# Turned queries and keys share the PSUM banks of the values; the values are spread over four units; the third pair's raw rows get a buffer

## The chip, the cores and the metric

The kernel runs on one core of one Trainium2 chip. The metric is device time in microseconds (us), the median of several executions; lower is better. TensorE is called PE here, VectorE DVE, ScalarE ACT, GpSimd POOL, and SyncE, which only issues DMAs, SP.

## The reference

Attention over 2 batches and 8 heads, 576 positions, head width 64, all fp32, with a bias made by a small network from the logarithmic distance of two positions; its output goes through a feed-forward layer with a rational activation and then through four experts. The change touches attention alone.

```
scores = scale * matmul(q, k.T)                # 16 (batch, head) pairs of 576 x 576
h = maximum(x @ w1 + b1, 0)                    # x from the distances, 32 hidden units
scores = scores + (h @ w2)                     # one bias per head
attn = exp(scores - max); attn /= sum
x = matmul(attn, v)                            # 576 x 64 for each (batch, head)
h = x @ w_in; g = P(h) / (Q(h) + 1e-6); x = g @ w_out
out = sum over 4 experts of p_e * (relu(x @ w1_e) @ w2_e)
```

## The kernel before

**Stages.** By the trace, the bias tables are made until 59 us of the span, attention runs from there to about 209 us, and the two feed-forward layers fill the rest. Everything is in an order written out by hand; each engine works through its own queue in that order, and waits only on semaphores.

**Attention** goes over 8 pairs of heads, n = 0 to 7. In a pair there are nine units, u = 0 to 8: a unit is 128 rows of scores of one head, and u = 8 holds the last 64 rows of both. For each unit PE makes scores (`sc`, line 453; units 2k and 2k+1 together), DVE adds the bias and takes the row extreme (`pq`, `nm`, line 457), ACT takes the exponential (line 466), and DVE turns the result in 32 x 32 blocks into `pt` (line 473). Scores run two units ahead of the turning. The values of pair n-1 (`o <- pt, val`, line 506, 18 blocks of 32 keys, 16 matmul records each) are made while pair n is at work, from `fill(n, u)`.

**PSUM.** `ps` has two tiles of two banks each, used in turn by all scores (one tile for each head of units 2k and 2k+1, one for u = 8) and by `rt`, the turned reciprocal sums (`turn`, lines 486 to 494), which ACT copies to `rs`. `po` has one tile of four banks, handed out by `big()`: once to `prep(n)`, which turns the raw queries and keys of pair n on PE (lines 172 to 181), and once to the values of a pair. Both take the same four banks by turns: a new owner waits until the old one's readers are done. `prep` puts its two ACT copies, to `ks` and `qs`, in the list `soon`, which runs after the turning in the next unit. `qs` and `ks` have two buffers each, so those of pair n+2 take the place of those of pair n. `divide` copies the finished values out of PSUM with three ACT instructions; `put` multiplies and splits them on POOL.

**Where these stand in pair n** (for n above 1): values at u = 1, 3 and 5, six blocks each; `divide` at u = 5; `turn` at u = 6; `prep(n + 2)` at u = 7, which at once has SP load the raw rows of pair n+3 into the single buffers `raw_q` and `raw_k`; `load_v(n + 1)` at u = 6 and the three copies of it within SBUF at u = 1 of the next pair. Pair 1 has 7, 7 and 4 blocks at u = 3, 5 and 6, and `prep(3)` at u = 8. `prep(1)` stands in pair 0 and `prep(2)` in pair 1 at u = 1; units 6 and 7 of pair 0 come after unit 1 of pair 1.

**SP's queue** is first in, first out. While the bias is made it takes the first pair's rows, the values, the second pair's rows, and then 32 transfers of the bias (`ba <- ev`, line 246); the rows of the third pair (`load_qk(2)`, issued by `prep(1)`) stand behind these.

**The feed-forward weights** of the first layer begin to be narrowed during pairs 4 to 7: three DVE instructions, two of ACT and one of POOL for each of four pieces.

Of the kernel before, what the change touches and what calls it, by code (L numbers as in the profile page):

```python
# [11 lines left out]
F32 = mybir.dt.float32  # L12
F32R = mybir.dt.float32r
U32 = mybir.dt.uint32
AF = mybir.ActivationFunctionType
# [3 lines left out]
B, H, S, D = 2, 8, 576, 64  # L19
# [6 lines left out]
P = 128  # L26
# [6 lines left out]
NKB = S // 32  # L33
# [14 lines left out]
def attention_then_two_ffn(ctx: ExitStack, tc: tile.TileContext, q, k, v, w1, b1, w2, w_in, w_out, ca, cb, probs, e_w1, e_w2, c_l, c_l8, c_p, c_x, out):  # L48
    nc = tc.nc
    act, dve, pool, pe, sp = nc.scalar, nc.vector, nc.gpsimd, nc.tensor, nc.sync  # L50
# [13 lines left out]
    ident = const.tile([P, P], F32, name="ident")  # L64
# [9 lines left out]
    def blk(slot, shape, dt, name):  # L74
        return long.tile(shape, dt, tag=f"blk{slot}", name=name)

    ps = ctx.enter_context(tc.tile_pool(name="ps", bufs=2, space=PSUM))
# [61 lines left out]

    raw_q = rp.tile([P, 5, 2, D], F32, name="raw_q")  # L140
    raw_k = rp.tile([P, 5, 2, D], F32, name="raw_k")
    val = [rp.tile([P, 2 * NKB, D], F32, tag=f"v{i}", name="val") for i in range(2)]

    def load_qk(n):

        p, b = divmod(n, 2)
        for x, y in ((raw_q, q), (raw_k, k)):
            h = y[b, 2 * p:2 * p + 2]
            for e in range(2):
                sp.dma_start(x[:, 0:4, e], h[e, 0:512].rearrange("(t p) d -> p t d", p=P))  # L150
            sp.dma_start(x[0:64, 4], h[:, 512:S].rearrange("e r d -> r e d"))
# [17 lines left out]
        for f in now:  # L169
            f()  # L170

    def turned(x, tp):
        for t in range(5):
            m = P if t < 4 else 64
            pe.transpose(tp[:, t * P:t * P + m], x[:m, t].rearrange("p e d -> p (e d)"), ident[:m, :m])  # L175

    def turn_q(n, tp):
        turned(raw_q, tp)

    def turn_k(n, tk):  # L180
        turned(raw_k, tk)

    def copy_q(n, tp):
        q_of[n] = qs = qk.tile([P, S], F32, tag="qs", name="qs")
        act.activation(qs, tp[:, :S], AF.Copy, scale=0.125)

    def copy_k(n, tk):
        k_of[n] = ks = qk.tile([P, S], F32, tag="ks", name="ks")
        act.activation(ks, tk[:, :S], AF.Copy)

    def prep_q(n, tp):
        turn_q(n, tp)
        copy_q(n, tp)

    def prep_k(n, tk):
        turn_k(n, tk)
        copy_k(n, tk)

    def two_banks():
        return ps.tile([P, 1024], F32, tag="s", name="tp_qk")  # L200

    bias = {}

# [60 lines left out]
    load_qk(0)  # L264
    load_v(0, 4)
    BESIDE = {0: cut_near, 2: lambda: inverse_psi(psi), 5: cut_far}
    BESIDE.update({6: lambda: prep_q(0, two_banks()), 7: lambda: (prep_k(0, two_banks()), load_qk(1))})
    for r in range(4):
        dve.tensor_scalar(wb[:, r], w2c, pick[:, 3 - r:4 - r], None, ALU.mult)
    for m in range(AHEAD):  # L270
# [151 lines left out]

    sums_z = ap.tile([P, P], F32, name="sums_z", bufs=1)

    def big():
        return po.tile([P, 4, 512], F32, tag="o", name="o")

    def prep(n):
        o = big().rearrange("p a j -> p (a j)")
        turn_q(n, o[:, 0:1024])  # L430
        turn_k(n, o[:, 1024:2048])
        if n + 1 < NN:
            load_qk(n + 1)
        soon.append(lambda: (copy_k(n, o[:, 1024:2048]), copy_q(n, o[:, 0:1024])))

    soon = []

    class Pair:
# [57 lines left out]
        def values(self, blocks):  # L496

            if blocks[0] == 0:
                self.o = big()
            for b in blocks:  # L500
                for a in range(4):
                    r = slice(32 * a, 32 * a + 32)
# [73 lines left out]
            act.activation(abs_b[:, j:j + 1], cb_sb[:, j:j + 1], AF.Abs, scale=WUP ** -(j + 1))  # L576
        dve.memset(one, 1.0 + 1e-6)

    VALUES = {1: range(0, 6), 3: range(6, 12), 5: range(12, NKB)}
    FIRST_VALUES = {3: range(0, 7), 5: range(7, 14), 6: range(14, NKB)}  # L580

    def fill(n, u):

# [1 line left out]
        turns = VALUES if n > 1 else FIRST_VALUES  # L585
        if old and u == 6:
            old.turn()
        if old and u in turns:
            old.values(turns[u])
        if old and u == max(turns):  # L590
# [4 lines left out]
            prep(1)  # L595
        if (n, u) == (1, 1):
            prep(2)
        if u == (7 if n > 1 else 8) and 0 < n < NN - 2:
            prep(n + 2)
        if u == 6 and 0 < n < NN - 1:  # L600
            load_v(n + 1)
        if (n, u) in COPY_V:
            copy_v(COPY_V[n, u])
# [283 lines left out]
```

## Time and profile before

| | before |
|---|---|
| median of 3 runs | 819.83 us (818.36 to 822.34) |
| the profiled execution, its own time | 817.92 us |
| its span on the core | 816.1 us |
| PE busy | 781.3 us, 96% |
| DVE busy | 463.3 us, 57% |
| ACT busy | 373.8 us, 46% |
| POOL busy | 132.0 us, 16% |

The span is the time from the first to the last instruction on the core; 1.8 us of the execution's own time lie around it. Shares over the span mix stages: DVE is nearly full until 400 us and almost idle later. A PE row covers a run of matmul records; each fp32 matmul leaves two. A row's end is modelled, and the next row begins before it ends. In square brackets stand the engine's idle time ahead of a row and what ended it; "issue" there means that nothing in the profile held the engine.

### The profile page before, as it was taken

The page shows a single profiled execution, that of the slowest core. Times are in us where ns is not written, and L with a number is a line of the kernel's source. Part 1 is how long each engine was busy: PE and PEld are TensorE (multiplying, and loading weights), DVE is VectorE, ACT ScalarE, POOL GpSimd, SP SyncE. Part 2 cuts the span into 40 slices and gives each one's busy share as a digit, 9 for nine tenths or more (in the row PEclk, how much of TensorE's full clock was granted, in tenths as well). Part 3 has the DMA queues.
Part 4 walks back from the last instruction along what each step waited for, and adds up shares of the span by engine and source line. Part 5 has one row for each costly group of instructions (what it writes and reads, how often), then busy time and mean ns, then how long its engine had stood idle before and what let it go on. Part 6 is the DMA issues. An engine that isn't in the chain of part 4 may idle for free.

```text
span 816.1 us, 15405 instructions
## 1 busy us (share of the span) xinstructions
PE 781.3 (96%) x6550; PEld 679.7 (83%) x6550; DVE 463.3 (57%) x707; ACT 373.8 (46%) x568; POOL 132.0 (16%) x111
## 2 busy tenths in 40 slices
PE   8996988988999999999989999999999999999998
PEld 5443766657899999999989989989899899898997
DVE  7986778787899999999963113322243112321211
ACT  6985555673798879886643113302022021210100
POOL 0000222343244546641200000000000000000000
PEclk9998899999999999999999999999999999999999
DMA  8898576542132233401213002200022000201001
GB/s 143 195 225 182 116 168 144 120 117 76 53 104 83 74 105 102 152 3 53 78 27 103 1 26 78 78 27 1 27 91 78 14 1 31 73 1 39 13 27 39
DMA packets 62179, 62.58 MB, mean 77 GB/s; under 512 B 36736, under 2 KB 45312, under 8 KB 61440
## 3 DMA queue, kind: packets, MB, share of 16 engines
q1 hardware_dynamic: 61680, 61.60, 28.4%
q8 instruction: 51, 0.84, 0.5%
q14 instruction: 16, 0.13, 0.1%
q10 hardware_dynamic: 432, 0.01, 0.0%
HBM read 42.43 MB, written 2.36 MB: 55 GB/s over the span
## 4 chain that ended last, share of the span: by engine, by line
PE 63%; DVE 14%; ACT 6%; issue 5%; POOL 2%; DMA 0%; SPq 0%; ACTq 0%; DVEq 0%; POOLq 0%
PE hp L56 26%; PE op L56 24%; PE sc L56 5%; PE o L506 5%; PE yp L56 2%; DVE qd L692 2%; DVE u L693 2%; DVE narrow L362 2%; DVE narrow L360 2%; DVE u L694 1%; PE o L175 1%; DVE hp L702 1%; DVE qd L701 1%; POOL wi L367 1%; ACT u L690 1%
## 5 line engine op out<-in xcount | busy, mean ns | idle before, releaser
L56 PE MATMUL hp<-x,wi 128*128 128x384 f32 x1656 | 295.6, 338 | 5.3 <-DVE u L703 4.9
L56 PEld LDWEIGHTS hp<-x,wi 128*128 128x128 f32 x1656 | 288.9, 189 | 8.9 <-issue 5.3
L56 PE MATMUL op<-w,h_hi 128*128 128x512 f32 (+1 forms) x592 | 178.5, 384 | 0.0
L772 ACT ACTIVATE h_hi<-hp 128x768 fp32r<-128x768 f32 x48 | 39.0, 812 | 246.6 <-PE hp L56 246.6
L773 DVE SCALAR_TENSOR_TENSOR h_lo<-hp,h_hi 128x768 fp32r<-128x768 f32 x48 | 46.0, 958 | 156.2 <-ACT h_hi L772 156.2
L56 PEld LDWEIGHTS op<-w,h_hi 128*128 128x128 f32 x592 | 110.0, 188 | 21.1
L56 PE MATMUL op<-w,h_lo 128*128 128x512 f32 (+1 forms) x296 | 113.7, 384 | 0.0
L56 PE MATMUL yp<-g_hi,w 128*128 128x384 f32 x384 | 102.1, 336 | 0.4 <-ACT y L756 0.4
L830 DVE SCALAR_TENSOR_TENSOR acc<-op,pr_sb,acc 128x512 f32<-128x512 f32 (+1 forms) x28 | 20.5, 732 | 112.9 <-PE op L56 112.9
L466 ACT ACTIVATE pq<-pq,nm 128x576 f32<-128x576 f32 x72 | 55.4, 770 | 38.1 <-DVE nm L457 37.8
L56 PEld LDWEIGHTS yp<-g_hi,w 128*128 128x128 f32 x384 | 69.7, 188 | 1.3 <-ACT y L756 0.7
L457 DVE CUSTOM_DVE_ANT_0 pq<-sc,ba 128x576 f32<-128x576 f32 x72 | 51.7, 750 | 30.4 <-PE sc L56 30.2
L56 PE MATMUL sc<-ks,qs 64*128 64x288 f32 (+1 forms) x320 | 60.6, 448 | 6.6 <-DVE nm L457 3.8
L56 PEld LDWEIGHTS op<-w,h_lo 128*128 128x128 f32 x296 | 55.6, 188 | 11.2
L56 PE MATMUL yp<-g_lo,w 128*128 128x384 f32 x192 | 64.2, 334 | 0.0
L506 PE MATMUL o<-pt,val 32*64 32x128 f32 (+1 forms) x2304 | 51.5, 307 | 9.9 <-issue 7.2
L506 PEld LDWEIGHTS o<-pt,val 32*64 32x64 f32 x2304 | 42.6, 137 | 20.3 <-issue 14.9
L683 POOL TENSOR_TENSOR g_lo<-u,g_hi 128x768 fp32r<-128x768 f32 x24 | 45.3, 1889 | 68.2 <-ACT g_hi L682 53.7
L56 PEld LDWEIGHTS sc<-ks,qs 64*128 64x128 f32 (+1 forms) x320 | 32.4, 185 | 24.7 <-DVE nm L457 10.7
L473 DVE STREAM_TRANSPOSE pt<-pq 128x576 f32<-128x576 f32 x72 | 52.5, 755 | 0.1
L233 PE MATMUL bps<-hid,wb 128*32 128x288 f32 x576 | 46.9, 410 | 3.8 <-DVE hid L222 2.9
L222 DVE TENSOR_SCALAR hid<-tab,cut 128x576 f32<-128x576 f32 x112 | 48.4, 516 | 0.0
(95 smaller groups left out, 793.2 us busy)
## 6 DMA issues: line engine op xcount, KB each, us to landing
stage<-in_moe_w_dram SPq DMA_DIRECT2D x32, 512.0 KB, 3.5
ba<-ev SPq DMA_DIRECT2D x32, 288.0 KB, 5.2
words<-in_moe_w_in_dram SPq DMA_DIRECT2D x8, 1024.0 KB, 5.6
words<-in_moe_w_out_dram SPq DMA_DIRECT2D x8, 1024.0 KB, 5.0
val<-val SPq DMA_DIRECT2D x21, 288.0 KB, 4.5
val<-in_v_dram SPq DMA_DIRECT2D x11, 288.0 KB, 4.1
raw_q<-in_q_dram SPq DMA_DIRECT2D x16, 128.0 KB, 2.9
raw_k<-in_k_dram SPq DMA_DIRECT2D x16, 128.0 KB, 2.9
```

Of the source, the lines that this page charges most:

```text
L56: pe.matmul(o, lhsT=l, rhs=r, start=start, stop=stop)
L222: dve.tensor_scalar(tiles[par], win, at, 0.0, ALU.add, ALU.max)
L233: pe.matmul(sc[32 * par:32 * par + 32, hf, :288], lhsT=wb.rearrange("p r h -> p (r h)"), rhs=tiles[par][:, 288 * hf:288 * hf + 288], start ...
L360: dve.scalar_tensor_tensor(out=u, in0=lo, scalar=29, in1=u, op0=ALU.logical_shift_right, op1=ALU.bitwise_or)
L457: dve.tensor_tensor_reduce(out=self.row(u + e).rearrange("p (a j) -> p a j", a=2), in0=o[:, :, :288], in1=bs.rearrange("p (a j) -> p a j", ...
L466: act.activation(self.row(u), self.row(u), AF.Exp, bias=least.pop((self.n, u)), scale=-1.0, accum_out=self.sm[:, u:u + 1])
L473: dve.transpose(self.pt[:, 5 * e + k], self.row(u))
L506: pe.matmul(self.o[64 * e:64 * e + 64, a, c:c + 32 * m], lhsT=val[self.n % 2][r, NKB * e + b], rhs=self.pt[r, i:i + m, 32 * b:32 * b + 32] ...
L683: pool.tensor_tensor(lo, u, f32(hi), ALU.subtract)
L772: act.activation(hi, h, AF.Relu)
L773: dve.scalar_tensor_tensor(out=lo, in0=h, scalar=0.0, in1=f32(hi), op0=ALU.max, op1=ALU.subtract)
L830: dve.scalar_tensor_tensor(out=acc[:, j, cols], in0=op, scalar=pr_sb[:, j, e:e + 1], in1=acc[:, j, cols], op0=ALU.mult, op1=ALU.add)
```

## The change

**PSUM.** The four banks of `po` become one tile `ob` for the whole of attention. The values keep columns 0 to 191 of each bank. The queries turned by `prep` go to columns 192 to 447 of banks 0 and 1, the keys to the same columns of banks 2 and 3, and the last 64 rows of each to columns 448 to 511 of banks 0 and 1. A matmul's start flag counts for a bank, so the transposes of pairs 3 and above, made while values are being summed there, carry none.

**Copies.** Queries and keys lie in two banks each, so `copied` takes three ACT instructions for each (256, 256 and 64 columns) where there was one of 576.

**Order.** Values stand at u = 1, 3, 5 and 7 with 5, 5, 3 and 5 blocks; in pair 1 at u = 3, 5 and 7 with 6, 4 and 8. `divide` moves with the last of them to u = 7, `prep(n + 2)` from u = 7 (pair 1: 8) to u = 5, ahead of that unit's values; `load_v(n + 1)` moves from u = 6 to u = 8.

**The third pair.** Its raw rows get a buffer of their own, `raw_2` (in a block of SBUF that later holds a part of attention's output), and `load_qk(2)` is issued right behind `load_qk(1)`, in the bias stage.

```diff
@@ -139,12 +139,17 @@
 
     raw_q = rp.tile([P, 5, 2, D], F32, name="raw_q")
     raw_k = rp.tile([P, 5, 2, D], F32, name="raw_k")
+    raw_2 = blk(10, [P, 2, 5, 2, D], F32, "raw_2")
+
+    def raw(n):
+        return (raw_2[:, 0], raw_2[:, 1]) if n == 2 else (raw_q, raw_k)
+
     val = [rp.tile([P, 2 * NKB, D], F32, tag=f"v{i}", name="val") for i in range(2)]
 
     def load_qk(n):
 
         p, b = divmod(n, 2)
-        for x, y in ((raw_q, q), (raw_k, k)):
+        for x, y in zip(raw(n), (q, k)):
             h = y[b, 2 * p:2 * p + 2]
             for e in range(2):
                 sp.dma_start(x[:, 0:4, e], h[e, 0:512].rearrange("(t p) d -> p t d", p=P))
@@ -169,35 +174,28 @@
         for f in now:
             f()
 
-    def turned(x, tp):
-        for t in range(5):
+    def turned(x, parts, start=True):
+        for t, out in enumerate(parts):
             m = P if t < 4 else 64
-            pe.transpose(tp[:, t * P:t * P + m], x[:m, t].rearrange("p e d -> p (e d)"), ident[:m, :m])
-
-    def turn_q(n, tp):
-        turned(raw_q, tp)
-
-    def turn_k(n, tk):
-        turned(raw_k, tk)
-
-    def copy_q(n, tp):
-        q_of[n] = qs = qk.tile([P, S], F32, tag="qs", name="qs")
-        act.activation(qs, tp[:, :S], AF.Copy, scale=0.125)
-
-    def copy_k(n, tk):
-        k_of[n] = ks = qk.tile([P, S], F32, tag="ks", name="ks")
-        act.activation(ks, tk[:, :S], AF.Copy)
-
-    def prep_q(n, tp):
-        turn_q(n, tp)
-        copy_q(n, tp)
-
-    def prep_k(n, tk):
-        turn_k(n, tk)
-        copy_k(n, tk)
-
-    def two_banks():
-        return ps.tile([P, 1024], F32, tag="s", name="tp_qk")
+            pe.matmul(out, lhsT=x[:m, t].rearrange("p e d -> p (e d)"), rhs=ident[:m, :m], is_transpose=True, start=start, stop=True, skip_group_check=True)
+
+    def copied(x, tp, tail, scale):
+        for a in range(2):
+            act.activation(x[:, 256 * a:256 * a + 256], tp[:, a], AF.Copy, scale=scale)
+        act.activation(x[:, 512:S], tail, AF.Copy, scale=scale)
+
+    def qs_tile(n):
+        q_of[n] = qk.tile([P, S], F32, tag="qs", name="qs")
+        return q_of[n]
+
+    def ks_tile(n):
+        k_of[n] = qk.tile([P, S], F32, tag="ks", name="ks")
+        return k_of[n]
+
+    def prep_first(x, to, scale):
+        tp = ps.tile([P, 1024], F32, tag="s", name="tp_qk")
+        turned(x, [tp[:, t * P:min(S, (t + 1) * P)] for t in range(5)])
+        act.activation(to, tp[:, :S], AF.Copy, scale=scale)
 
     bias = {}
 
@@ -264,7 +262,7 @@
     load_qk(0)
     load_v(0, 4)
     BESIDE = {0: cut_near, 2: lambda: inverse_psi(psi), 5: cut_far}
-    BESIDE.update({6: lambda: prep_q(0, two_banks()), 7: lambda: (prep_k(0, two_banks()), load_qk(1))})
+    BESIDE.update({6: lambda: prep_first(raw_q, qs_tile(0), 0.125), 7: lambda: (prep_first(raw_k, ks_tile(0), 1.0), load_qk(1), load_qk(2))})
     for r in range(4):
         dve.tensor_scalar(wb[:, r], w2c, pick[:, 3 - r:4 - r], None, ALU.mult)
     for m in range(AHEAD):
@@ -422,16 +420,15 @@
 
     sums_z = ap.tile([P, P], F32, name="sums_z", bufs=1)
 
-    def big():
-        return po.tile([P, 4, 512], F32, tag="o", name="o")
+    ob = po.tile([P, 4, 512], F32, tag="o", name="o")
 
     def prep(n):
-        o = big().rearrange("p a j -> p (a j)")
-        turn_q(n, o[:, 0:1024])
-        turn_k(n, o[:, 1024:2048])
-        if n + 1 < NN:
+        q_tail, k_tail = ob[:, 0, 448:512], ob[:, 1, 448:512]
+        for x, a, tail in zip(raw(n), (0, 2), (q_tail, k_tail)):
+            turned(x, [ob[:, a + t // 2, 192 + P * (t % 2):320 + P * (t % 2)] for t in range(4)] + [tail], n < 3)
+        if 1 < n < NN - 1:
             load_qk(n + 1)
-        soon.append(lambda: (copy_k(n, o[:, 1024:2048]), copy_q(n, o[:, 0:1024])))
+        soon.append(lambda: (copied(ks_tile(n), ob[:, 2:4, 192:448], k_tail, 1.0), copied(qs_tile(n), ob[:, 0:2, 192:448], q_tail, 0.125)))
 
     soon = []
 
@@ -496,7 +493,7 @@
         def values(self, blocks):
 
             if blocks[0] == 0:
-                self.o = big()
+                self.o = ob[:, :, 0:192]
             for b in blocks:
                 for a in range(4):
                     r = slice(32 * a, 32 * a + 32)
@@ -576,8 +573,8 @@
             act.activation(abs_b[:, j:j + 1], cb_sb[:, j:j + 1], AF.Abs, scale=WUP ** -(j + 1))
         dve.memset(one, 1.0 + 1e-6)
 
-    VALUES = {1: range(0, 6), 3: range(6, 12), 5: range(12, NKB)}
-    FIRST_VALUES = {3: range(0, 7), 5: range(7, 14), 6: range(14, NKB)}
+    VALUES = {1: range(0, 5), 3: range(5, 10), 5: range(10, 13), 7: range(13, NKB)}
+    FIRST_VALUES = {3: range(0, 6), 5: range(6, 10), 7: range(10, NKB)}
 
     def fill(n, u):
 
@@ -585,6 +582,8 @@
         turns = VALUES if n > 1 else FIRST_VALUES
         if old and u == 6:
             old.turn()
+        if u == 5 and 0 < n < NN - 2:
+            prep(n + 2)
         if old and u in turns:
             old.values(turns[u])
         if old and u == max(turns):
@@ -595,9 +594,7 @@
             prep(1)
         if (n, u) == (1, 1):
             prep(2)
-        if u == (7 if n > 1 else 8) and 0 < n < NN - 2:
-            prep(n + 2)
-        if u == 6 and 0 < n < NN - 1:
+        if u == 8 and 0 < n < NN - 1:
             load_v(n + 1)
         if (n, u) in COPY_V:
             copy_v(COPY_V[n, u])
```

SP at the end of the bias stage, before. `raw_q` and `raw_k` are the raw rows, `ba` the bias, `ev` its source; the first four rows load pair 1, the last two begin pair 2:

```order
L150 DMA raw_q<-in_q_dram 128x4x64 x2
L151 DMA raw_q<-in_q_dram 64x2x64
L150 DMA raw_k<-in_k_dram 128x4x64 x2
L151 DMA raw_k<-in_k_dram 64x2x64
L246 DMA ba<-ev 128x1x576 x32
L150 DMA raw_q<-in_q_dram 128x4x64 x2
L151 DMA raw_q<-in_q_dram 64x2x64
```

The same place after; `raw_151` is the new buffer:

```order
L155 DMA raw_q<-in_q_dram 128x4x64 x2
L156 DMA raw_q<-in_q_dram 64x2x64
L155 DMA raw_k<-in_k_dram 128x4x64 x2
L156 DMA raw_k<-in_k_dram 64x2x64
L155 DMA raw_151<-in_q_dram 128x4x64 x2
L156 DMA raw_151<-in_q_dram 64x2x64
L155 DMA raw_151<-in_k_dram 128x4x64 x2
L156 DMA raw_151<-in_k_dram 64x2x64
L244 DMA ba<-ev 128x1x576 x32
```

The six transfers of pair 2 have moved from behind the 32 of the bias to ahead of them.

PE from unit 8 of pair 2 into pair 3, before: the scores of u = 8, `rt`, the first scores of pair 3, the turned rows of pair 4, the next scores, then values:

```order
L56 MATMUL sc<-ks,qs 64x288 x4
L491 MATMUL rt<-ident,rb 128x128 x4
L56 MATMUL rt<-fold,sums_z 128x64
L56 MATMUL sc<-ks,qs 128x288 x4
L175 MATMUL o<-ident,raw_q 128x128 x4
L175 MATMUL o<-ident,raw_q 128x64
L175 MATMUL o<-ident,raw_k 128x128 x4
L175 MATMUL o<-ident,raw_k 128x64
L56 MATMUL sc<-ks,qs 128x288 x4
L506 MATMUL o<-pt,val 64x160
```

The same place after:

```order
L503 MATMUL o<-pt,val 64x160
L56 MATMUL sc<-ks,qs 64x288 x4
L488 MATMUL rt<-ident,rb 128x128 x4
L56 MATMUL rt<-fold,sums_z 128x64
L56 MATMUL sc<-ks,qs 128x288 x4
L503 MATMUL o<-pt,val 64x160
L503 MATMUL o<-pt,val 64x128
```

Between the first two scores of a pair now stand five blocks of values, and the transposes have gone to the far side of u = 8.

ACT over the same place, before (`x_1528` is what `divide` writes, `pq` the exponential):

```order
L519 ACTIVATE x_1528<-o 128x4x4x32
L519 ACTIVATE x_1528<-o 64x64 x2
L466 ACTIVATE pq,sm<-pq,nm 128x576
L494 ACTIVATE rs<-rt 128x576
L466 ACTIVATE pq,sm<-pq,nm 128x576 x2
L189 ACTIVATE ks<-o 128x576
L185 ACTIVATE qs<-o 128x576
```

and after:

```order
L184 ACTIVATE ks<-o 128x256 x2
L185 ACTIVATE ks<-o 128x64
L184 ACTIVATE qs<-o 128x256 x2
L185 ACTIVATE qs<-o 128x64
L491 ACTIVATE rs<-rt 128x576
L463 ACTIVATE pq,sm<-pq,nm 128x576
L516 ACTIVATE x_1592<-o 128x4x4x32
L516 ACTIVATE x_1592<-o 64x64 x2
```

The copies to `ks` and `qs` have moved ahead of the copy to `rs`, and the three copies of `divide` behind it.

## Rows read from the trace of the kernel before

**Rows 1.** PE around `prep(2)`: start, us, line, output, count, idle before.

```profile
74.81 0.83 PE L175 MATMUL o<-ident,raw_q 128*128 128x128 f32 x5 [1.75 <-DMA raw_q<-in_q_dram]
77.35 1.38 PE L175 MATMUL o<-ident,raw_k 128*128 128x128 f32 x5 [1.71 <-DMA raw_k<-in_k_dram]
...
81.62 2.96 PE L56 MATMUL sc<-ks,qs 64*128 64x288 f32 x8 [0.86 <-DVE nm L457]
84.51 3.36 PE L506 MATMUL o<-pt,val 32*64 32x160 f32 x112
```

**Rows 2.** SP from the bias stage on, same columns.

```profile
28.09 41.11 SPq L246 DMA_DIRECT2D ba<-ev  x32
69.31 3.19 SPq L150 DMA_DIRECT2D raw_q<-in_q_dram  x2
```

**Rows 3.** DVE around `prep(2)` and at the end of attention.

```profile
74.38 1.43 DVE L473 STREAM_TRANSPOSE pt<-pq 128x576 f32<-128x576 f32 x2
80.80 0.76 DVE L457 CUSTOM_DVE_ANT_0 pq<-sc,ba 128x576 f32<-128x576 f32 x1 [4.99 <-PE sc L56]
...
194.28 2.35 DVE L473 STREAM_TRANSPOSE pt<-pq 128x576 f32<-128x576 f32 x3
```

**Rows 4.** Windows: busy us of each engine, granted PE clock, DMA share, GB/s.

```profile
77.40:87.00 9.60, 8.74 (x104) 6.41 (x108) 5.81 (x14) 4.45 (x10) 1.02 (x3) 0.50 0.58 124
109.60:126.40 16.80, 14.52 (x344) 10.47 (x344) 12.83 (x30) 10.05 (x25) 4.82 (x8) 1.00 0.67 165
139.40:141.60 2.20, 0.00 (x1) 0.00 (x0) 2.19 (x5) 0.52 (x2) 0.00 (x0) 0.99 0.00 0
141.60:143.70 2.10, 2.08 (x44) 1.64 (x46) 0.00 (x0) 0.08 (x1) 0.00 (x0) 0.50 0.04 8
163.00:179.00 16.00, 14.59 (x344) 10.15 (x344) 14.09 (x33) 11.05 (x26) 6.52 (x9) 1.00 0.47 122
196.70:199.60 2.90, 2.86 (x80) 2.50 (x80) 1.80 (x4) 0.00 (x0) 2.46 (x4) 0.50 0.03 6
```

**Rows 5.** PE in pairs 2 to 4.

```profile
99.31 1.91 PE L506 MATMUL o<-pt,val 32*64 32x160 f32 x96 [1.05 <-ACT qs L185]
...
118.29 1.24 PE L56 MATMUL sc<-ks,qs 64*128 64x288 f32 x8 [1.95 <-DVE pt L473]
...
124.39 1.19 PE L56 MATMUL sc<-ks,qs 64*64 64x288 f32 x8
...
126.44 1.94 PE L56 MATMUL sc<-ks,qs 64*128 64x288 f32 x8
...
131.24 1.91 PE L506 MATMUL o<-pt,val 32*64 32x160 f32 x96 [0.25 <-ACT qs L185]
```

**Rows 6.** ACT in pair 3.

```profile
126.45 0.65 ACT L494 ACTIVATE rs<-rt 128x576 f32<-128x576 f32 x1
...
130.00 0.65 ACT L189 ACTIVATE ks<-o 128x576 f32<-128x576 f32 x1 [0.29 <-PE o L175]
130.55 0.64 ACT L185 ACTIVATE qs<-o 128x576 f32<-128x576 f32 x1
```

**Rows 7.** ACT's groups by shape: busy us, mean ns, idle before.

```profile
L749 ACT ACTIVATE yacc<-yp 128x384 f32<-128x384 f32 x12 | 4.8, 488 | 0.0
...
L519 ACT ACTIVATE x<-o 64x64 f32<-64x64 f32 x14 | 3.0, 212 | 0.1
```

**Rows 8.** PE's waits from 84 to 200 us: total us, times, longest.

```profile
PE o L506 <- issue: 7.2, 5, 2.4
```

**Rows 9.** DMA queues from 138.09 to 141.62 us: packets, MB, share.

```profile
q1 hardware_dynamic: 32, 0.15, 20.2%
q8 instruction: 1, 0.02, 1.6%
```

**Rows 10.** PE at the end of attention.

```profile
190.53 1.91 PE L506 MATMUL o<-pt,val 32*64 32x160 f32 x96
...
196.74 2.97 PE L506 MATMUL o<-pt,val 32*64 32x160 f32 x80 [2.43 <-issue]
```

## The prediction

> **What bounds the kernel now.** PE is busy for 96% of the span, so I read first what PE does in attention, the one stage that the change touches, and which waits it has there. What attention saves or loses reaches the end of the kernel: the work behind it is in fixed order and PE or DVE has no slack to give back. I read PE's rows around the third pair, then two steady pairs, then the waits that nothing explains, then the end.
>
> Around `prep(2)` PE stands idle for 1.75 us until the raw queries are there and 1.71 us more for the keys [rows 1]. These loads were issued at 69.31, behind 32 transfers of the bias that kept SP for 41.11 us [rows 2]. DVE, done at 75.81, then waits 4.99 us for scores [rows 3]. From 77.4 to 87.0 the granted clock is 0.50, the lower of PE's two levels, 1.2 GHz [rows 4]: two tiles of scores take 2.96 us and the values, 112 records, 3.36 [rows 1], where a full clock gives 1.24 and, for 96 records, 1.91 [rows 5].
>
> In a steady pair PE is nearly full, and three small things hold it: values wait for the copy of the turned queries (1.05 us in pair 2, about 0.25 in each of four pairs), the first scores of a pair take 1.94 us instead of 1.24 because their second half waits for `rs`, and now and then PE waits for nothing that the profile shows. That last sort makes 7.2 us in 5 times [rows 8], of which the 2.43 us at 196.74 [rows 10] is no such wait: the last transposes end at 196.63 [rows 3] and the values read them. So 4.8 us are left; I add the 1.95 us at 118.29, put down to transposes that these scores don't read [rows 5]: 6.7 us. In the longest, 139.4 to 141.6, PE is idle and the clock falls to 0.50 afterwards [rows 4]; hardly anything moves but one transfer of the instruction queue [rows 9].
>
> **The change part by part.** Sums go against the profiled execution, 817.92 us (span 816.1), which is 1.9 us under the median; I carry the difference over to the median.
>
> *The third pair's rows.* Six transfers move ahead of the bias. With the rows there, PE goes on at 73.06 (74.81 less 1.75): turning, at most twice 0.83, to 74.7; two tiles of scores to 75.9. DVE ends its transposes at 75.81, and then has two extremes (0.76 each) and two transposes (1.43): 78.8. The values need those transposes, so they begin at 78.9 instead of 84.51: 5.6 us. What is next late is DVE. At a full clock their 112 records take 2.2 us (1.91 for 96) instead of 3.36: 1.15. Together **-6.8** (bounds -6.0 and -7.5: DVE a little later or earlier). Cost: 576 KB, as much as two of the bias transfers, which take 41.11/32 = 1.3 us each. The bias may come 2.6 us later; I cost that at nothing, as DVE waits for PE alone in this stretch [rows 3]; what it costs otherwise is a rival.
>
> *Own columns for the values.* Their start no longer waits for the copies: 1.05 + 4 x 0.25 = 2.1. The transposes on DVE are next late, by some 0.1 us a time; I take **-1.6**.
>
> *Copies ahead of `rs`.* The buffers of pair n+2 are those of pair n, which the scores of u = 8 read last. The copies now stand in ACT's queue right where these scores are made, so they start when the scores end, at 124.39 + 1.19 = 125.6 in pair 3 [rows 5]; queued behind them are `rs`, the exponential of u = 8 and `divide`, and the first scores of the next pair wait for `rs`. A copy of 576 columns takes 0.55 us from start to start and 0.65 by itself [rows 6], so 0.10 overlaps. 384 columns take 0.49 [rows 7], less 0.10 is 0.39; by the slope between the two, 256 columns take 0.28. 64 columns take at most 0.21 [rows 7]. Six copies: 2 x (2 x 0.28 + 0.21) = 1.5 us. `rs` starts at 127.1 instead of 126.45: 0.65 later. (The exponential that stood ahead of it has moved up, since `divide` is out of its way.) Five pairs: **+3.2**. Bounds: without overlap 1.9 us, +1.1 a pair, +5.5; at the price of two copies 1.1 us, +0.25 a pair, +1.2.
>
> By the Trainium skill, "ScalarE: Activation LUTs", section "What ACT_TABLE_LOAD costs", an instruction with constant scale and bias costs 186 ns and 0.833 ns a column, less some 93 ns of overlap: an estimate of 1.52 us for the six and +3.3 for the five pairs, so page and rows agree within 0.1.
>
> *Later pairs.* From 163 to 179 DVE is busy 14.09 of 16.0 us [rows 4], because the weights are narrowed there; a later start of a pair's scores has less room to be made up. **+1.0**, between 0 and 2.
>
> *Three units become four.* The work on PE is the same: 18 blocks, ten transposes. `divide` now follows the values of u = 7 and stands ahead of the next pair's first exponential; its cover is that the exponential's reader, the transpose, comes two tiles of scores later. POOL's `put` and the value loads shift by some units and have as many to spare.
>
> *The end.* In the last pair only three blocks stand ahead of the scores of u = 8, six before: half of 1.91 [rows 10], 0.9 us earlier, of which the five blocks and `divide` that now follow take back 0.4, as the last values must wait for that. Those five blocks fill the pause of 2.43 us, which shrinks to some 1.3. After the pause the clock is 0.50 [rows 4] and 80 records take 2.97 us instead of 1.6; after PE's 1.95 us at 118.29 it stayed at 1.00 [rows 4]. **-0.5 - 1.4 = -1.9**; without the clock -0.5. `put` of pair 6 starts later with `divide`; the first feed-forward matmuls read it only in their last quarter, and begin themselves with the last values, so I cost it at nothing; if it is late, it eats into the 1.9.
>
> *The unexplained waits.* All 6.7 us lie in or next to runs of values. Before, the rows of pair n+3 and the three copies of the values follow one another on SP and meet three runs of six blocks. After, the copies wait for a load issued two units later, and the rows come behind them: both fall on u = 3 to 8, and the runs are shorter. No row shows what this does: from none left (-6.7) to as many again (+6.7). I take the half, **-3.4**, because the one wait whose DMAs I looked at ends with a transfer of instructions that came late.
>
> The Trainium skill, "Runtime: NRT & Kernel Launch", section "Instruction fetch mechanics", says that crossing a block of instructions is mostly hidden by the prefetch. By that rule these waits are not of fetching, nothing here would change them, and the sum lacks the -3.4; the trace speaks against it with the 2.2 us in which PE is idle [rows 4] and one such transfer runs [rows 9].
>
> Sum: -6.8 - 1.6 + 3.2 + 1.0 - 1.9 - 3.4 = **-9.5 us**: 808.4 for an execution like the profiled one, 810.3 against the median.
>
> **The rivals.**
>
> *The unexplained waits stay as they are.* For it: their number may hang on the count of instructions alone, which hardly changes. Against it: the transfers that they sit beside move. -6.1: 813.7. This is the result of the skill's rule above.
>
> *The copies bind the pair.* Copies without overlap (+5.5), the narrowing stretch at its worst (+2), the clock at the end falls again (-0.5), waits as before: -6.8 - 1.6 + 5.5 + 2 - 0.5 = -1.4: 818.4, no change. For it: PE and ACT both wait at one point, five times over. Against it: the copies before did overlap [rows 6].
>
> *The third pair's rows are no gift.* The bias, 2.6 us later, holds up DVE in pair 0 by as much: 812.9. For it: SP is full for 41.11 us [rows 2]. Against it: DVE waited for no DMA there.
>
> *Slower: PE is held in its values.* Copies of values and raw rows now come in one row behind a later load; if they hold up what PE needs in u = 3 to 8, each further wait costs 2.2 us and a stretch of 2.1 us at half clock, 1.05 more [rows 4], 3.2 in all. Two of them eat the 6.1; four make 819.83 - 6.1 + 12.8 = 826.5. It decides from the fourth on. For it: such waits exist. Against it: the runs of values get shorter.
>
> **How the numbers follow.** The forecast has a chance of 0.50, the waits as they are 0.25, the copies bind 0.12, the rows no gift 0.08, slower 0.05. The predicted time is the forecast's, 810.3. The range goes down to 805, where nearly all the unexplained waits and the half clock behind them are gone, and up to 817, which takes in 812.9 and 813.7 with the upper bounds of two terms; it leaves out most of "the copies bind" and the slower case. Within 0.5%, 4.1 us, is about what a measurement can't tell from no change. Faster by more: 0.50 + 0.25 + 0.08 less 0.04 for upper bounds that add up, 0.79; the same: 0.12 + 0.04 = 0.16; slower: 0.05.
>
> **What would show it.** In the profile after: no DMA ends an idle stretch of PE at `prep(2)`, and no low clock from 77 to 87 us; the values of pair 1 begin at 79 us. No values row waits for `qs`. `rs` starts 1.5 us after the scores of u = 8, and the first scores of a pair take about 2.5 us. Six copies take 1.5 us. The last values are no longer at half clock. "Issue" waits of PE come to about half of 6.7 us. I am wrong if the scores of pair 1 wait for the bias, if the six copies take 1.9 us or more, or if "issue" waits grow.

## The result, and the profile after

| | before | after |
|---|---|---|
| median | 820.68 us, 4 runs (818.36 to 822.34) | 808.95 us, 4 runs (808.74 to 809.10) |
| the profiled execution | 817.92 us | 809.1 us |
| its span | 816.1 us | 807.3 us |
| mean granted clock | 0.987 | 0.994 |

The ratio is 0.9859 (95% interval 0.9832 to 0.9885), 11.7 us less; the forecast was 810.3, with 805 to 817. Profile against profile the gain is 8.8 us where the sum said 9.5. On a second chip, where the changed kernel ran again beside the experiments, it took 808.12 us (806.04 to 811.46), a ratio of 0.9886 (0.9837 to 0.9935) to the kernel before. Ratios leave disturbed executions out; among the experiments that concerns two of four runs of `e1_third_buffer`, the profiled one among them, and one of ten of `e9_buffer_warm`.

The 8.8 us, by PE's rows: the first scores of pair 2 begin at 89.36 (94.26 before), 4.9 us; from there to the first scores of pair 7 it is 81.65 us (84.82), 3.2; from there to the first feed-forward matmuls 19.48 (20.57), 1.1; behind them 0.4 is lost.

PE around `prep(2)` after, answering to [rows 1] (start, us, line, output, count, idle before):

```profile
69.36 1.23 PE L56 MATMUL sc<-ks,qs 64*128 64x288 f32 x6 [0.82 <-DVE nm L454]
70.98 2.87 PE L56 MATMUL sc<-ks,qs 64*128 64x288 f32 x8 [0.39 <-DVE nm L454]
73.78 2.75 PE L180 MATMUL o<-ident,raw 128*128 128x128 f32 x10
76.18 2.38 PE L56 MATMUL sc<-ks,qs 64*128 64x288 f32 x8
79.42 1.91 PE L56 MATMUL sc<-ks,qs 64*128 64x288 f32 x8 [0.86 <-DVE nm L454]
81.26 2.07 PE L503 MATMUL o<-pt,val 32*64 32x160 f32 x96
```

No DMA stands in a bracket any more. But ten transposes take 2.75 us and the scores 2.38: half clock, as the windows show (busy us of each engine, granted clock, DMA share, GB/s), while the end of attention, answering to [rows 4], is at full clock:

```profile
61.80:71.80 10.00, 7.93 (x46) 4.37 (x46) 8.70 (x22) 7.32 (x23) 0.00 (x0) 1.00 0.98 221
71.80:78.60 6.80, 6.76 (x24) 4.02 (x24) 4.03 (x8) 4.03 (x13) 0.00 (x0) 0.50 0.83 175
184.20:190.50 6.30, 5.17 (x183) 3.86 (x175) 6.13 (x12) 3.93 (x10) 1.49 (x2) 1.00 0.30 112
```

ACT and PE where pair 3 meets pair 4, answering to [rows 5, 6]: the scores of u = 8 end at 120.37 + 1.19 = 121.56, six copies take 122.89 - 121.61 = 1.28 us, and `rs` starts 1.33 us after the scores (0.87 before).

```profile
120.37 1.19 PE L56 MATMUL sc<-ks,qs 64*64 64x288 f32 x8
...
122.42 0.75 PE L56 MATMUL sc<-ks,qs 64*128 64x288 f32 x2
123.64 1.23 PE L56 MATMUL sc<-ks,qs 64*128 64x288 f32 x6 [0.47 <-ACT rs L491]
```

```profile
121.61 0.66 ACT L184 ACTIVATE ks<-o 128x256 f32<-128x256 f32 x2 [1.33 <-PE sc L56]
122.15 0.23 ACT L185 ACTIVATE ks<-o 128x64 f32<-128x64 f32 x1
122.25 0.68 ACT L184 ACTIVATE qs<-o 128x256 f32<-128x256 f32 x2
122.78 0.27 ACT L185 ACTIVATE qs<-o 128x64 f32<-128x64 f32 x1
122.89 0.71 ACT L491 ACTIVATE rs<-rt 128x576 f32<-128x576 f32 x1
```

PE's waits from 84 to 200 us (total, times, longest), answering to [rows 8]; no row of values waits for `qs` now. Of the 2.1 us of "issue", the 0.50 at 175.51 in pair 7 is a wait for DVE, whose transposes end at 174.65 + 0.77 = 175.42; 1.6 us are left:

```profile
PE sc L56 <- DVE nm L454: 3.2, 6, 0.9
PE sc L56 <- ACT rs L491: 2.4, 5, 0.7
PE o L503 <- issue: 2.1, 4, 0.9
PE o L503 <- ACT x L516: 1.1, 1, 1.1
```

The end, answering to [rows 10]: a pause of 1.12 us instead of 2.43, then 1.64 us for 80 records instead of 2.97.

```profile
188.92 1.64 PE L503 MATMUL o<-pt,val 32*64 32x160 f32 x80 [1.12 <-ACT x L516]
```

### The profile page after: what moved, and what is told of

Same layout as the page of the kernel before. It is cut to its first block, busy times and chain, and to the rows that moved or that the text cites. A ratio compares the mean times of both kernels' runs of the same rounds, so it can differ in the third digit from the quotient of the medians.

```text
span 807.3 us, 15423 instructions
## 1 busy us (share of the span) xinstructions
PE 780.8 (97%) x6550; PEld 677.1 (84%) x6550; DVE 464.7 (58%) x707; ACT 374.3 (46%) x596; POOL 132.3 (16%) x111
## 4 chain that ended last, share of the span: by engine, by line
PE 63%; DVE 16%; ACT 7%; issue 4%; POOL 2%; DVEq 0%; ACTq 0%; POOLq 0%
PE hp L56 27%; PE op L56 24%; PE sc L56 5%; PE o L503 3%; PE yp L56 3%; DVE narrow L358 2%; DVE qd L689 2%; DVE narrow L360 2%; DVE u L690 2%; PE o L180 1%; DVE pq L454 1%; DVE pt L470 1%; DVE u L691 1%; DVE narrow L356 1%; DVE hp L699 1%
## 5 line engine op out<-in xcount | busy, mean ns | idle before, releaser
L503 PE MATMUL o<-pt,val 32*64 32x160 f32 (+1 forms) x2304 | 48.5, 293 | 3.3 <-issue 2.1
L503 PEld LDWEIGHTS o<-pt,val 32*64 32x64 f32 x2304 | 39.2, 130 | 13.3 <-issue 7.8
```

Of the source, the lines that this page charges most:

```text
L503: pe.matmul(self.o[64 * e:64 * e + 64, a, c:c + 32 * m], lhsT=val[self.n % 2][r, NKB * e + b], rhs=self.pt[r, i:i + m, 32 * b:32 * b + 32] ...
```

## The experiments

Three questions were open: what the third pair's rows are worth by themselves and why their 6.8 us came short; what took PE's waits that nothing in the profile explains from 6.7 to 1.6 us; and what the copies ahead of `rs` and the four units do. Each kernel ran beside the kernel before, whose median was 817.3 to 819.6 on the three chips; each has one profile, which need not lie at its median.

### The third pair's rows and the clock

**e1_third_buffer**: the buffer alone, on the kernel before.

```
+    raw_2 = blk(10, [P, 2, 5, 2, D], F32, "raw_2")
...
-        for x, y in ((raw_q, q), (raw_k, k)):
+        for x, y in zip(raw(n), (q, k)):
...
-    ... 7: lambda: (prep_k(0, two_banks()), load_qk(1))
+    ... 7: lambda: (prep_k(0, two_banks()), load_qk(1), load_qk(2))
```

> The kernel before with one part of the change alone: the third pair's raw rows in a buffer of their own, loaded ahead of the bias. Theory A, the gift at the start stands by itself: the first scores of pair 2 begin at about 89.5 us (94.26 before, 89.36 after the whole change), so 817.92 less 4.7 = 813.2 in the profile, 0.994 of before. The predicted 6.8 us came short because the clock still falls; so a stretch at 0.50 should lie between 70 and 80 us here too. Rival B, the gift is the whole of the gain, and the rest of the change comes to nothing: 809 to 810, 0.987. Rival C, the rest of the change is needed for it (the turned rows of pair 2 still take the banks that the values want): pair 2 begins no earlier than 92, at most 2.3 us won, 0.997 to 1.000.

**e2_no_third_buffer**: the changed kernel without it.

```
-    raw_2 = blk(10, [P, 2, 5, 2, D], F32, "raw_2")
...
-        return (raw_2[:, 0], raw_2[:, 1]) if n == 2 else (raw_q, raw_k)
+        return raw_q, raw_k
```

> The changed kernel without the third pair's buffer: its rows are loaded behind the bias again. Theory A: the first scores of pair 2 begin at about 94 us, the intervals between the later pairs are those of the changed kernel, and it takes 809.1 + 4.7 = 813.8, 0.992 of before. Rival B, the buffer is the whole gain: 818 to 820, 0.998 to 1.002. Rival C, the other part can hide the late rows: 809 to 811.

`e1` ran in 806.82, 810.59, 819.47 and 820.15 us, at mean granted clocks of 0.998, 0.996, 0.981 and 0.981: median 815.03, ratio 0.9891 (0.9807 to 0.9976) from the two quicker. That settles none of A, B and C. `e2` took 813.05 (812.52 to 816.69), ratio 0.9963 (0.9936 to 0.9989), near A's 813.8, and its pairs last as long as those of the changed kernel (15.52, 16.13, 16.32 and 16.14 us for pairs 3 to 6, there 15.52, 16.13, 16.31 and 16.15), so the buffer acts on the start alone. The profiles show more. `e1`, profiled at 819.47, with the buffer:

```profile
77.60 2.75 PE L180 MATMUL o<-ident,raw 128*128 128x128 f32 x10
...
85.08 2.34 PE L511 MATMUL o<-pt,val 32*64 32x160 f32 x112
```

`e2`, without it:

```profile
77.43 1.41 PE L179 MATMUL o<-ident,raw_q 128*128 128x128 f32 x5
78.77 1.41 PE L179 MATMUL o<-ident,raw_k 128*128 128x128 f32 x5
...
84.90 2.07 PE L502 MATMUL o<-pt,val 32*64 32x160 f32 x96
```

Both begin the values that are made in pair 1 at 85 us, and neither waits for a DMA. In both the clock is 0.5 already from 62 to 69 us and again from 72 to 82, so PE comes to `prep(2)` late enough for rows loaded behind the bias. With the clock down that early, the buffer saves nothing in these two profiles; the two quicker runs of `e1` have none.

**e3_warm**: the changed kernel, with the pauses of pairs 0 and 1 filled.

```
             k, n = u // 2, self.n
+            for _ in range({(0, 2): 3, (1, 0): 4, (0, 6): 2}.get((n, u), 0)):
+                pe.transpose(ob[:, 0, 192:320], ident, ident)
```

> The changed kernel with nine further transposes of the unit matrix, into unused columns of the values' banks, in the pauses of pairs 0 and 1 (three, four and two of them). Nothing is left out. Theory A, the clock falls at 71.8 us because PE has little to do in the 10 us ahead of it, although no pause is longer than 0.9 us: with the pauses filled the granted clock stays at 1.00 from 72 to 79 us, the ten transposes take 1.6 us instead of 2.75, the scores behind them 1.24 instead of 2.38, the values of pair 1 begin 1.5 to 2.5 us earlier, and the kernel takes 806.5 to 807.6. Rival B, DVE binds this stretch and the clock is only seen beside it: the clock stays up but the time doesn't, 809 to 809.3. Rival C, the clock falls whatever PE does here: the fillers take PE's time at half clock, 809.3 to 811.

806.38 us (805.07 to 807.16), ratio 0.9861 (0.9798 to 0.9923); 806.44 in the profile, 2.7 under the changed kernel's. The medians don't part the two: they ran on different chips, and the changed kernel's ratios, 0.9859 and 0.9886, lie inside this interval. So the 2.7 rests on the profiles. The granted clock stays up, and the same ten transposes take 1.65 us:

```profile
62.00:69.00 7.00, 6.10 (x38) 3.48 (x36) 6.11 (x13) 5.30 (x16) 0.00 (x0) 1.00 0.97 218
69.00:72.00 3.00, 2.79 (x14) 1.64 (x15) 2.83 (x8) 2.02 (x5) 0.00 (x0) 1.00 0.94 234
72.00:82.40 10.40, 9.62 (x144) 6.51 (x141) 10.19 (x25) 6.79 (x21) 1.01 (x3) 1.00 0.71 147
```

```profile
72.65 1.65 PE L180 MATMUL o<-ident,raw 128*128 128x128 f32 x10
...
78.03 2.07 PE L505 MATMUL o<-pt,val 32*64 32x160 f32 x96
```

Theory A holds, with a time just under its range: the values made in pair 1 begin at 78.03 (81.26), the 78.9 that the prediction had for a full clock, and a little less.

**e10_rest_warm**: `e3` without the buffer, so the two diffs above together.

> The changed kernel without the third pair's buffer, with the same nine further transposes. Set against the changed kernel with them (806.4) it gives the worth of the buffer when the clock doesn't fall ahead of it. Theory A, with PE quick the raw rows are late again: PE waits for the raw queries and then the keys at prep(2), the values of pair 1 begin at about 82 to 83 us (78.0 with the buffer), and the kernel takes 810 to 811.5. Rival B, the rows are there in time or DVE hides them: 806.3 to 807.5. Rival C, the wait of PE lets the clock fall behind it: 812 to 813.

815.1 us (813.41 to 818.64), on another chip than `e3`: above all three. With PE quick, the rows are late again, and the clock falls behind the wait:

```profile
74.94 1.39 PE L179 MATMUL o<-ident,raw_q 128*128 128x128 f32 x5 [2.25 <-DMA raw_q<-in_q_dram]
76.61 1.39 PE L179 MATMUL o<-ident,raw_k 128*128 128x128 f32 x5 [0.28 <-DMA raw_k<-in_k_dram]
...
83.77 3.50 PE L504 MATMUL o<-pt,val 32*64 32x160 f32 x96
```

A's wait and C's clock come together: half clock from 74.2 to 87.9, the first scores of pair 2 at 93.61 instead of 86.13. This kernel also had a wait of 2.2 us in pair 2 (see `e5` below). So at a clock that holds until the rows are wanted, the buffer brings the values made in pair 1 forward by 83.77 - 78.03 = 5.7 us, and what follows by 7.5. Of the 5.7, the waits for the rows are 2.25 + 0.28 = 2.5; the rest is the half clock behind them.

### The rest of the change at a clock that is held

**e9_buffer_warm**: `e1` with the nine transposes; set against `e3` it lacks the rest of the change.

```
+            idle = {(0, 2): 3, (1, 0): 4, (0, 6): 2}.get((n, u), 0)
+            if idle:
+                extra = big()
+                for _ in range(idle):
+                    pe.transpose(extra[:, 0, 192:320], ident, ident)
```

> The kernel before with the third pair's buffer, and with nine further transposes of the unit matrix in the pauses of pairs 0 and 1, which hold the clock up there; nothing else of the change. Set against the changed kernel with the same further transposes (806.4) it gives the worth of the rest of the change at a clock that is held. Theory A, the rest is worth 4 us by itself, of which most is waits that nothing explains: 810 to 812, with 5 to 7 us of such waits and a scatter of some us among the runs. Rival B, the rest is worth nothing, and the changed kernel was only luckier with its clock: 806 to 807.5.

811.85 us, as A has it, with the scatter: 807.07 to 819.28 in 10 runs. `e3` is at 806.38, on another chip. Three waits of 1.44, 0.93 and 1.95 us (4.3 together, under A's 5 to 7) stand beside the last pause:

```profile
111.17 0.50 PE L516 MATMUL o<-pt,val 32*64 32x128 f32 x8 [1.44 <-issue]
...
152.76 0.52 PE L516 MATMUL o<-pt,val 32*64 32x128 f32 x13 [1.95 <-issue]
...
192.00 2.97 PE L516 MATMUL o<-pt,val 32*64 32x160 f32 x80 [2.43 <-issue]
```

Behind the 1.95 the clock is at half from 154.0 to 164.3. The quickest of the ten, 807.07 at a mean clock of 0.999, is 2 us above `e3`'s quickest (805.07), while the medians lie 5.5 apart: by this, most of what the rest is worth is waits and the clock behind them.

### The unexplained waits

**e4_before_no_values**: the kernel before; pairs 2 to 7 neither load nor copy values, and use those of pairs 0 and 1.

```
-        if u == 6 and 0 < n < NN - 1:
-            load_v(n + 1)
...
-    COPY_V.update({(n, 1): n for n in range(2, NN)})
```

> The kernel before; the values of pairs 2 to 7 are not loaded and not copied within SBUF, so those pairs use the values of pairs 0 and 1; PE's instructions are the same. Theory A, the waits that nothing in the profile explains (6.7 us in pairs 2 to 7) come from transfers of PE's instructions that start late beside the copies of the values: they fall under 2 us, the clock no longer falls at 141.6, and the kernel takes 817.9 less 5 to 7 = 811 to 813. Rival B, they hang on the count of instructions alone: 5 to 7 us of them are left and the time is 816 to 819. Rival C, it is the raw rows that they meet: fewer of them, 3 to 5 us, at other places.

812.36 us, ratio 0.9936 (0.9906 to 0.9966), 5.0 us under the kernel before: A. In the profile, the slowest of the eight runs, the waits are down to 2.7 us from 6.7 (0.86, 0.85, 0.27 and 0.74), though not under 2, with PE's instructions unchanged, and no low clock at 141 us (one stands at 176.6 to 183.4):

```profile
PE o L506 <- issue: 1.9, 3, 0.9
...
PE sc L56 <- issue: 0.9, 1, 0.9
```

**e12_load_late**: the kernel before, one load moved.

```
-        if u == 6 and 0 < n < NN - 1:
+        if u == 8 and 0 < n < NN - 1:
             load_v(n + 1)
```

> The kernel before with one thing moved: the load of the next pair's values is issued at u = 8, as after the change, and not at u = 6. Theory A, the unexplained waits come from where the values' copies stand in time, beside PE's instruction transfers: 2 to 3.5 us of them are left (6.7 before) and the kernel takes 812 to 815. Rival B, the place of this load doesn't matter, it is the raw rows that were moved to u = 5, or the length of the runs: 5 to 7 us of waits, 815 to 819.

815.62 us, ratio 0.9960 (0.9931 to 0.9989), 3.9 us under the kernel before on that chip. The waits, without the last pause of 2.43, are 0.38, 0.23 and 0.85, and 1.41 put down to transposes like the 1.95 of [rows 5]: 2.9 us, as A expected. The profile is that of the quickest of the eight runs. The median lies in B's range, 0.6 us above A's; set against the kernel before on that chip it is 3.9 less, nearly the 3.8 us of waits that are gone.

```profile
PE o L506 <- issue: 3.9, 4, 2.4
PE sc L56 <- DVE pt L473: 1.4, 1, 1.4
```

One moved load takes away more than half of the waits: SP used to send the three copies right behind the raw rows (132.70 behind 131.96), and now they wait for the load (135.68, the load at 131.30).

**e7_double**: `e3` with twice the copies.

```
-        for a in range(1, 4):
+        for a in (1, 2, 3, 1, 2, 3):
             sp.dma_start(val[n % 2][32 * a:32 * a + 32], val[n % 2][0:32])
```

> The changed kernel with the nine further transposes, and with each pair's three copies of the values within SBUF issued twice, the second time with the same result. Nothing is left out. Theory A, transfers beside PE's instruction transfers cause the unexplained waits: they grow from 2.4 us to 4 to 6 us, at runs of values near the copies, 808 to 811. Rival B, they hang on the count of instructions: 2 to 2.5 us and 806 to 807. Rival C, the doubled copies come too late for the values, and PE waits for a copy in every pair: 2 us each, 815 or more.

814.27 us. Neither A nor C alone: in the profile (818.64, the slowest of eight runs) "issue" waits are 3.5 us, less than A's 4 to 6, with one of 2.11 us and 0.50 that is a wait for DVE, and in pair 2 alone the values wait for copies:

```profile
PE o L505 <- DMA val<-val: 3.8, 3, 2.5
PE o L505 <- issue: 3.5, 3, 2.1
```

### The copies and the four units

**a_after** and **e5_rs_between**, on one chip: the changed kernel as it is, and with the copies to `qs` behind `rs`.

```
-        soon.append(lambda: (copied(ks_tile(n), ...), copied(qs_tile(n), ...)))
+        soon.append(lambda: copied(ks_tile(n), ...))
+        (behind if n > 2 else soon).append(lambda: copied(qs_tile(n), ...))
...
         if old and u == 6:
             old.turn()
+            catch_up(behind)
```

> The changed kernel as it is, beside the others of this chip. 808 to 810, and hardly any scatter. The clock: it may fall for 6.8 us somewhere between 60 and 85 us, as it did at 71.8, since PE has little to do there; where the fall takes twice as long, 812 or more.

> The changed kernel with the three copies to qs moved behind the copy to rs on ACT (from pair 3's rows on); the three to ks stay ahead. Nothing is left out. Theory A, the copies ahead of rs are what makes the first scores of a pair take 2.45 us: rs starts 0.87 us after the scores of u = 8 end instead of 1.33, PE's wait for rs (2.4 us in five times) falls to about 0.3, and the kernel takes 1.5 to 2.3 us less than the changed one, 806.7 to 807.5. Rival B, DVE or the values behind bind the pair and the wait comes back there as another: within 0.5 us of the changed kernel. Rival C, the three copies behind rs hold the exponential of u = 8 and divide, and the next pair's values wait: 1 to 3 us more.

808.12 (806.04 to 811.46, so with more scatter than expected) and 808.14 us (804.04 to 809.74): by the medians B, no difference. By the profiles A: the wait for `rs` is gone,

```profile
122.86 1.19 PE L56 MATMUL sc<-ks,qs 64*64 64x288 f32 x8
...
124.92 1.86 PE L56 MATMUL sc<-ks,qs 64*128 64x288 f32 x8
```

and pairs 3 to 6 last 14.93, 15.55, 15.65 and 15.54 us, some 0.6 less each than 15.53, 16.13, 16.32 and 16.14 in `a_after`. Profile against profile the kernel is 1.7 us quicker (809.74 against 811.46), not 2.4, since pair 2 begins 1.0 us earlier but lasts 19.99 us against 18.28: it has a longer wait, which the first trace of the changed kernel doesn't have, and half clock for 3.4 us behind it, from 100.0. Half clock further ahead is no difference: 10.2 us from 69.2 here, 6.8 and 3.4 in `a_after`. Why the medians of four runs each show nothing is not shown beyond that; the quickest, at 0.998 and 0.997 of the clock, are 2.0 us apart.

```profile
98.28 1.57 PE L504 MATMUL o<-pt,val 32*64 32x128 f32 x68 [2.37 <-DMA val<-val]
```

In `a_after` this wait takes 1.68. In pair 1 `prep(3)` now stands ahead of the copies of its values, and SP issues the raw rows of pair 4 first.

**e11_three_runs**: `e3` with three runs of six blocks from pair 2 on, and so `divide` at u = 5.

```
-    VALUES = {1: range(0, 5), 3: range(5, 10), 5: range(10, 13), 7: range(13, NKB)}
+    VALUES = {1: range(0, 6), 3: range(6, 12), 5: range(12, NKB)}
```

> The changed kernel with the nine further transposes, and with one part undone: from pair 2 on the values stand in three runs of six blocks at u = 1, 3 and 5, with divide at u = 5, as before the change. Theory A, only the end is lost: the pause ahead of the last values is 2.4 us again, the unexplained waits stay at 1 to 2.4 us, and the kernel takes 1.3 us more than with four runs (806.4), or 2.7 with a fall of the clock behind the pause: 807.5 to 809.2. Rival B, it is the shorter runs that took the unexplained waits away: they come to 5 to 7 us again, with a fall of the clock behind the longest, 811 to 814.

827.55 us, ratio 1.0122 (1.0084 to 1.0161): slower than before the change, and neither theory. "Issue" waits are 0.9 us, so the length of the runs doesn't make them. In the profile, the quickest of six runs, it is `rs`:

```profile
139.34 0.93 ACT L518 ACTIVATE x<-o 128x512 f32<-128x512 f32 x3 [1.27 <-PE o L505]
140.30 0.63 ACT L364 ACTIVATE w<-narrow 128x512 fp32r<-128x512 f32 x1
140.84 0.76 ACT L465 ACTIVATE pq<-pq,nm 128x576 f32<-128x576 f32 x1
...
141.71 0.66 ACT L184 ACTIVATE ks<-o 128x256 f32<-128x256 f32 x2
...
142.99 0.71 ACT L493 ACTIVATE rs<-rt 128x576 f32<-128x576 f32 x1
```

`divide`, which waits for the values of u = 5, stands ahead of the last exponential and the six copies; `rs` starts 2.75 us after the scores of u = 8 (139.05 + 1.19 on PE), and PE's waits for it, 2.3 us in `e3`, come to this, with half clock after three of them:

```profile
PE sc L56 <- ACT rs L493: 6.4, 5, 1.9
```

**e13_best**: `e3` and `e5` together, and the copies of pair 1's values ahead of the raw rows.

```
+        if (n, u) == (1, 5):
+            copy_v(1)
         if u == 5 and 0 < n < NN - 2:
             prep(n + 2)
...
-    COPY_V = {(1, 5): 1}
+    COPY_V = {}
```

> The changed kernel with three things: the nine further transposes in the pauses of pairs 0 and 1, the copies to qs behind the copy to rs, and the copies of the values of pair 1 ahead of prep(3)'s raw rows on SP. Nothing is left out. Theory A, three costs of the changed kernel are separate and add up: the clock at the start (2.6 us), the wait for rs (0.6 us a pair, 2.4 us), and in some executions a wait of 1.7 to 2.4 us in pair 2 for the values' third copy, which stands on SP behind raw rows: 803 to 804.5, 0.983 to 0.985 of before, granted clock 0.998 or more, and no wait of PE for a copy of the values. Rival B, taking one away makes another late (DVE binds the pairs): 805.5 to 807.

802.01 us (800.90 to 805.10), ratio 0.9799 (0.9771 to 0.9826): A, and 1 us better. So the three costs add up, and by its ratio this version beats both kernels. The profile's mean clock is 1.00, pairs 2 to 6 last 15.97, 14.94, 15.54, 15.65 and 15.54 us, and from 84 to 200 us one "issue" wait is left in attention's pairs, 0.50 us for DVE's transposes, and none for a copy:

```profile
PE sc L56 <- DVE nm L457: 3.8, 6, 1.0
PE o L506 <- issue: 1.2, 2, 0.7
PE o L506 <- ACT x L519: 1.1, 1, 1.1
```

## Why the prediction was right

The time was right, and the sum within 0.7 us of the profile, but by errors that cancelled.

**The third pair's rows, -6.8: mis-sized, 4.9 measured.** The mechanism was right: no DMA wait, the values made in pair 1 earlier (5.6 predicted; 5.7 between `e10` and `e3`, more than half of it the clock), DVE next. The step that failed is "a full clock". The prediction took the low clock at 77 for a consequence of the waits for raw rows, but it falls at 71.8 behind pauses of at most 0.86 us, so transposes and scores ran at half clock and the values began at 81.26, not at 78.9. `e3` shows the other 3.2 us: with the pauses filled the first scores of pair 2 begin at 86.13, 8.1 us earlier than before. The bias starts at 31.65 instead of 28.09 [rows 2], 3.6 us later, and held nothing up: no wait of PE or DVE in pair 0 names it. SP's row after:

```profile
31.65 41.63 SPq L244 DMA_DIRECT2D ba<-ev  x32
```

**Own columns, copies, later pairs: -1.6 + 3.2 + 1.0 = +2.6; about +4.0 measured.** The 3.2 us won from pair 2 to 7 hold 5.4 of unexplained waits (6.76 less the 1.33 in those pairs after) and 1.7 of the clock (half of the stretch from 141.6 to 145.0), so the rest lost 4.0. Of it the copies cost 0.6 us a pair in four pairs of `e5`, which moves the three to `qs` alone; an estimate for five pairs is 3.0 (3.2 predicted; the wait for `rs` shows 2.4 of it). What own columns give and later pairs cost leaves +1.0 where -0.6 was expected; no run parts the two. The traces show that the waits of values for `qs`, 2.1 us in these pairs, are gone, and that PE waits for DVE's `nm` instead, 2.3 us where it was none: 1.8 of that in pair 6, where DVE is busy 14.5 of 16.2 us, as the prediction feared for later pairs. The six copies took 1.28 us; the rows had given 1.5, and by the estimate from the Trainium skill, "ScalarE: Activation LUTs", section "What ACT_TABLE_LOAD costs", 1.52: the trace shows less than either.

**Three units become four, costed at nothing: the rest hangs on it.** It is in the prediction's aside that `divide` is out of the exponential's way: where the values stand in three runs and `divide` stays at u = 5 (`e11` undoes the two together), the profile is 13.4 us longer than `e3`'s, and the median, on another chip, 21. That is the rival "the copies bind", which the spreading keeps away; its price in the prediction, +5.5 for copies without overlap, left out the queue ahead of the copies and the clock behind.

**The unexplained waits, -3.4: -5.1 measured.** Right in direction, and for the reason given, the place of the values' copies beside the raw rows: `e12` moves one load and loses 3.8 of 6.7, `e4` takes the copies and loads away and loses 4.0, `e11` changes the runs and gains none. That half would go was a guess, as the prediction says.

That instructions arrive late was argued from one wait; the kept traces show it for all. Count PE's records (weight loads, matmuls, semaphore instructions) from the start of a trace: each of the 40 unexplained waits that the fourteen profiles have between 84 and 200 us (37 "issue", 3 put down to transposes) ends where the count so far leaves 193 when divided by 256, so they lie at the joints of blocks of 256 instructions. Each ends 1.2 to 1.8 us after a 16 KB transfer of the instruction queue has ended; the longest, up to 141.62, has that of [rows 9], from 139.33 to 140.21. The other "issue" waits, four of the pause ahead of the last values and eight of 0.50 us in pair 7, stand at no joint and end with DVE's transposes. In the profile before, the transfer ahead of the four waits above 1 us started 6.3, 3.9, 2.4 and 7.4 us after the joint before it, and 0.4 to 2.0 MB of other transfers had begun by then; in the six blocks where under 10 KB had, it started within 1.4 us. After the change it starts 4.0 us late at most. No run changed the instruction transfers alone.

The Trainium skill, "Runtime: NRT & Kernel Launch", section "Instruction fetch mechanics", has such crossings mostly hidden. The traces agree with "mostly": PE waits at five of 20 joints before and at three of 20 after. The prediction's step from there, that these waits are not of fetching, is what they contradict.

The prediction also left out of its sum that with the longest wait the low clock behind it goes, 1.7 us, though it had seen it [rows 4].

**The end, -1.9: 1.1 measured**, as the pause and the clock came out as said (1.12 us, full clock) and 0.7 of waits came into pair 7, 0.5 of them for DVE.

**The slower rival** named its mechanism rightly, copies and raw rows in one row on SP, but it costs one wait in pair 2, in some executions (1.68 in `a_after`).

## What to carry to other kernels

Before a stall is costed as a gain, look whether the clock ahead of it is safe: in single profiles the same buffer was worth 0, 3.3 or 5.7 us at the values made in pair 1 (the 3.3 with the rest of the change), by when PE's clock fell, and nine idle transposes in short pauses kept it up until the rows were wanted. When work is put ahead of a small copy that an engine waits for, ask what stands ahead of it in that queue and waits itself; moving `divide` and the last values by two units was worth more than any edit with a price. When an engine waits in the middle of a run of its own work and nothing is named, count its instructions between such waits: here they were multiples of 256, and what came late was the instructions. And where a kernel scatters from run to run, compare pairs in the profiles too, since the medians of four runs hid 2.4 us that four pairs show.

## What was not expected of the hardware

PE's clock fell to 0.50 with no pause above 0.86 us since 20 us of the span, at times between 61.9 and 71.8 us from one execution to the next, of kernels whose PE work is alike up to there. It stayed there for 6.8 to 10.2 us, and longer where PE then waited for raw rows (13.6 in `e12`). Nine transposes that nobody reads, 1.6 us of PE's time, kept it at 1.00 there in all six kernels that have them, until one of these waited for the rows. That is a part of the scatter, not all of it: the runs of `e1` lie 13 us apart and those of `e3` 2.1, but those of `e9`, with the same nine transposes, 12. Where copies within SBUF were issued right behind raw rows, PE waited up to 2.2 us for its instructions, although it reads neither at that moment; with the load moved, up to 1.4 (`e12`).
